# The first MLP pieces by token tile, means ahead of variances, bias transposes ahead: one change at the seam between attention and MLP of batch 0

## The chip, the cores and the metric

The kernel runs on one core of a Trainium2 chip. The metric is the device time of one execution in microseconds (us). The comparison of before and after is by medians over several runs; the profile describes one execution.

## The reference, cut to what matters

Attention over 8 batches of 8 heads, 576 positions, 64 wide, with a causal mask and a bias that comes from a running sum over `s`; then, for each token of 512 values, a LayerNorm, a two-layer MLP (512 to 2048 to 512, ReLU between) and a residual sum.

```python
scores = scale * q @ k.T                       # (8, 8, 576, 576)
cum = np.cumsum(np.maximum(s, 0.0), axis=-1)
bias = -(cum[:, :, :, None] - cum[:, :, None, :])
scores = np.where(causal, -1e9, scores + np.minimum(bias, 0.0))
x = softmax(scores) @ v                        # heads side by side: (8, 576, 512)
mu, var = x.mean(-1), ((x - mu) ** 2).mean(-1)
xn = (x - mu) / np.sqrt(var + 1e-6) * g_ln
out = x + np.maximum(xn @ w_ch1, 0.0) @ w_ch2
```

## The kernel before, in words

**Order of the work.** One loop over the 64 heads, `n = 8 b + h` (L732), is written out by hand: the schedule is manual, each engine runs its instructions in the order in which the loop issues them, and a semaphore wait of one instruction holds back all behind it on that engine. A step of the loop issues the scores of head `n` on TensorE (`scores`, L300: three PSUM tiles `sa`, `sb`, `sc`, each followed by an exponential on ScalarE into `er`; `scores_d`, L337, for every second head the small corner tile `sd`), two or more MLP "units" of the batch before (`run_units`, L544), and the product with `v` of an earlier head (`pv_next`, L717, which runs `pv`, L374: 15 small matmuls into `pot`, then a reciprocal and two scalings on VectorE into `xb` and `xm`). In steps 0 to 7 there is no MLP work yet, since batch 0 has to be complete first. `keep_warm` (L552) issues matmuls on zeros into a tile `idle`; nothing uses them.

**MLP units.** `batch_units` (L526) makes 32 units for each batch: 16 of `mlp1` (L480), which take 128 of the 2048 hidden columns each, four matmuls of 128x128 weights `w_bf` by 512 tokens `xT` into a tile `ph`, and a ReLU into `hT` on ScalarE (or on VectorE for the first unit of a step); then 16 quarters of `mlp2` (L498) into `py`, where each fourth one ends with the scaling by `rstd`, the residual sum into `yo` and the store.

**LayerNorm.** `ln_stats` (L414) takes partial statistics of the finished heads' columns; `ln_xn` (L439) merges them for one token tile (`bn_aggr` into `mv`) and makes `xn = (x - mean) * g`; with `on_pool` the two steps of `xn` run on GpSimd (`xc`, then `xn`). The division by the deviation is not in `xn`: it is applied after `mlp2` through `rstd`, which works since ReLU lets a positive factor through. `ln_tr` (L465) transposes `xn` on TensorE (`trx`) and copies it to `xT`. For batch 0, `pv_next` at its last head runs all four tiles: tile 3 on GpSimd, tiles 0 to 2 on VectorE, then `rstd`. Step 8 (L757) issues the scores of head 8, one warm-up matmul, all four `ln_tr`, then three units of all 512 tokens.

**Queries and keys.** For the first three batches they come as pairs of heads: `ld_cast_pair` (L129, GpSimd's DMA queue) loads them as `kp` and `qp`, `tr_pair` (L239) transposes them on TensorE into `trqk`, `evac_pair` (L258) copies them into `kq`, the keys on VectorE and the queries on ScalarE, two copies each. The table `PAIRS` (L659) says at which step which pair is made; in steps from 9 on, `qk_pair` (L271) stands behind the first two units. Pair `g` serves heads `2g` and `2g + 1`: pair 5 made in step 9 serves head 10 on.

**The bias rows.** `bias_rows` (L221) transposes the running sums to token-major form, 15 small transposes into `trc` and four copies on ScalarE into `cT`, at step 12. `cT` is first read by `cast_rows` at step 19.

**PSUM.** Pool `ps_s` holds three banks (`sa`, `sb`, `sc`), `ps_m` two (`ph`, `py`, and `trqk` up to pair 4), `ps_t` two (`trx`, `sd`, `idle`, later `trqk`, and `pot` of batch 0's odd heads), `ps_o` one (`pot`).

**GpSimd's queue** also issues the weight loads: `pre` (L662) places the loads of pairs 6 and 7 and of two quarters of `w2` at step 8, the other two quarters at step 10. Behind them stand the causal selects (`affine_select`, L327) of heads from 10 on.

Of the kernel before, what the change touches and what calls it, by code (L numbers as in the profile page):

```python
# [9 lines left out]
F32 = mybir.dt.float32  # L10
BF16 = mybir.dt.bfloat16
# [4 lines left out]
P = 128  # L16
# [3 lines left out]
def kernel(  # L20
# [54 lines left out]
    hT = const.tile([P, FB, 512], BF16, name="hT")  # L75
    gb = const.tile([P, Dm], F32, name="gb")
    rstd = const.tile([P, B, NT], F32, name="rstd")
    mhalf = const.tile([P, 8], F32, name="mhalf")
    v_bf = [const.tile([P, NT, H, D + 1], BF16, name=f"v_bf{i}") for i in range(2)]

# [137 lines left out]
                in_=src[0:m, :].unsqueeze(1).to_broadcast([m, G - a, S]),  # L218
            )

    def bias_rows():  # L221
        tr = ps_t.tile([P, 3, NT, BH], BF16, name="trc", tag="tr")
        for j, src in enumerate((c_hi, c_mid, c_lo)):
            for t in range(NT):
                pn = P if t < NF else TL
                nc.tensor.transpose(
                    tr[0:pn, j, t, :], src[:, t * P : t * P + pn], ident[0:BH, 0:BH]
                )
        for t0, t1, pn in ((0, NF, P), (NF, NT, TL)):
# [4 lines left out]
            nc.scalar.copy(out=cT[0:pn, t0:t1, 1, :, 0], in_=tr[0:pn, 0, t0:t1, :])  # L234


    trs = {}
# [186 lines left out]
    xTs = {}  # L424
    xns = {}

    done = {}
# [5 lines left out]
    def ln_rstd(b):  # L433
        n = len(x_tiles(b))
        rs = rstd[:, b, 0:n]
        nc.vector.tensor_scalar_add(out=rs, in0=mvs[b][:, 0:n, 1], scalar1=1e-6)  # L436
        nc.gpsimd.tensor_tensor(out=rs, in0=rs, in1=mhalf[:, 0:n], op=ALU.pow)  # L437

    def ln_xn(b, t, on_pool=False):  # L439
        tiles = x_tiles(b)  # L440
        if t >= len(tiles):
            return
        nc.vector.bn_aggr(out=mvs[b][:, t, :], in_=st[b][:, t, 0 : 4 if b == 0 else 3, :])  # L443
        xn = xnp.tile([P, Dm], BF16, name="xn", tag="xn")
        if on_pool:
            xc = yop.tile([P, Dm], F32, name="xc", tag="yo")
            nc.gpsimd.tensor_scalar(
                out=xc, in0=tiles[t], scalar1=mvs[b][:, t, 0:1], scalar2=None, op0=ALU.subtract
            )
            nc.gpsimd.tensor_tensor(out=xn, in0=xc, in1=gb, op=ALU.mult)  # L450
        else:
            nc.vector.scalar_tensor_tensor(  # L452
                out=xn,
                in0=tiles[t],
                scalar=mvs[b][:, t, 0:1],
                in1=gb,
                op0=ALU.subtract,
                op1=ALU.mult,
            )
        xns[b, t] = xn  # L460
        done[b] = done.get(b, 0) + 1
        if done[b] == len(tiles):
            ln_rstd(b)

    def ln_tr(b, t, eng="dve"):  # L465
        if (b, t) not in xns:
            return
        xn = xns.pop((b, t))
        tr = ps_t.tile([P, KD, P], BF16, name="trx", tag="tr")
        for kd in range(KD):  # L470
            nc.tensor.transpose(tr[:, kd, :], xn[:, kd * P : (kd + 1) * P], ident)  # L471
# [80 lines left out]
    def keep_warm(n):  # L552
        w = ps_t.tile([P, 512], F32, name="idle", tag="tr")
        for _ in range(n):
            nc.tensor.matmul(w, lhsT=zeros[:, 0:P], rhs=zeros, start=True, stop=True)
# [99 lines left out]

    PAIR_LOADS = {12: 8, 13: 9, 14: 10, 17: 11}
    PAIRS = {9: 5, 11: 6, 13: 7, 14: 8, 15: 9, 16: 10, 21: 11}  # L659


    def pre(n):  # L662
        if n == 0:
            nc.vector.memset(mhalf, -0.5)
            ld_cast_pair(4)
        elif n == 1:
            ld_w1(1)
        elif n == 3:
            ld_cast_pair(5)
            for t in range(NT):  # L670
                ld_cast_v(1, t)
        elif n == 4:
            ld_w1(2)
            ld_w1(3)
        elif n == 8:
            ld_cast_pair(6)
            ld_w2(0)
            ld_cast_pair(7)
            ld_w2(1)
        elif n == 10:  # L680
            ld_w2(2)
            ld_w2(3)
        elif n == 12:
            bias_rows()
            nc.vector.memset(cT[:, :, 0, :, 0], -1.0)
            nc.vector.memset(cT[:, :, 1, :, 1:4], 1.0)
        elif n == 16:
            for r in rows:
                nc.gpsimd.memset(r[:, :, :, KA:P], 0.0)
        if n in PAIR_LOADS:  # L690
            ld_cast_pair(PAIR_LOADS[n])
        if n % 4 == 0 and 2 <= n // 4 + 1 < 2 * NPE:
            aug(n // 4 + 1, nc.sync)
        for gam in range(2 * NPE, NG):
            m = n - 4 * gam
            if m == -6:
                ld_rows(gam, 0), ld_rows(gam, 1)
            elif m == -5:
                cast_rows(gam, 0), cast_rows(gam, 1)
                ld_rows(gam, 2), ld_rows(gam, 3)  # L700
            elif m == -4:
                tr_rows(gam, 0), tr_rows(gam, 1)
                cast_rows(gam, 2), cast_rows(gam, 3)
                ld_rows(gam, 4)
            elif m == -3:
                tr_rows(gam, 2), tr_rows(gam, 3)
                cast_rows(gam, 4)
            elif m == -2:
                tr_rows(gam, 4)
        for nb in range(2, B):  # L710
            m = n - H * nb + (5 if nb == 2 else 7)
            if 0 <= m < NT:
                ld_v(nb, m)
            if 1 <= m <= NT:
                cast_v(nb, m - 1, "pool")

    def pv_next():  # L717
        pb, ph_ = pend.pop(0)
        pv(pb, ph_)
        if ph_ in (3, 5) or (ph_ == 7 and pb > 0):  # L720
            ln_stats(pb, ph_ // 2 - 1)
        elif pb == 0 and ph_ in (6, 7):
            ln_stats(0, ph_ - 4)
        if ph_ == 7:
            ln_open(pb)
            if pb == 0:
                ln_xn(0, 3, True)
            for t in range({0: 3, 1: 2, B - 1: 1}.get(pb, NT)):
                ln_xn(pb, t)


    for n in range(BH):  # L732
        b, h = n // H, n % H
        pre(n)
        if n < 8:
            scores(b, h)
            if h in (1, 3, 5, 6):
                scores_d(b, h // 2)
            if h in (0, 2, 4):
                qk_pair(h // 2 + 1, ("dve", "dve"), ("act", "dve" if h < 4 else "act"))  # L740
            pend.append((b, h))
            if n == 7:
                pv_next()
                tr_pair(4)
                pv_next()
                evac_pair("k", 4, ("act", "act"))
                evac_pair("q", 4, ("act", "act"))
                keep_warm(4)
                continue
            if n % 2 == 1 or n == 0:  # L750
                keep_warm(2)
            if n > 1:
                pv_next()
            if n == 6:
                pv_next()
            continue
        if n == 8:  # L757
            scores(b, h)
# [12 lines left out]
        run_units(1, True)  # L771
        if h % 2 == 0:
            scores_d(b, h // 2)
        run_units(1)
        if n in PAIRS:
            qk_pair(PAIRS[n], ("dve", "dve"), ("act", "act"))
        if n > 9:
            pv_next()
        pend.append((b, h))
        lt = {2: (0, 1), 3: (2, 3, 4)}.get(h, ()) if b > 1 else ()  # L780
        for t in lt:
            ln_tr(b - 1, t)
            if t != 1 and t != 4:
                run_units(1)
                nu -= 1
        if n == 2 * H + 2:
            for t in range(2, NT):
# [46 lines left out]
```

## Time and profile before

| | before |
|---|---|
| median of 13 runs | 378.62 us (377.14 to 381.52) |
| the profiled execution: device time | 378.97 us |
| its span in the trace | 377.2 us |
| mean granted TensorE clock | 0.982 |
| TensorE (PE) busy with matmuls | 362.5 us, 96% of the span |
| VectorE (DVE), ScalarE (ACT), GpSimd (POOL) busy | 205.4, 194.1, 166.1 us |
| bytes moved by DMA | 50.42 MB |

How to read the lines of the trace that follow below: a line of the timeline gives start and duration in us, then engine, source line, operation, output and inputs by the program's names, shapes and a count; `x4` is four instructions merged, and the duration then runs from the first one's start to the last one's end. In brackets stands how long the engine had been idle just before and what ended it. A single matmul shows its whole passage through the array (some 0.2 to 0.4 us), of which the next one overlaps most: prices are taken from start to start. A line of the stages gives, for each stretch, its length, the busy time of PE, weight loads, DVE, ACT and POOL with counts, the granted clock (1.00 is full), and DMA.

### The profile page before, as it was taken

Reading aid. Unit: us, or ns where it says so; the run is one execution under the profiler, and the core shown is the slowest. Engines: PE = TensorE matmul, PEld = TensorE weight load, DVE = VectorE, ACT = ScalarE, POOL = GpSimd, SP = SyncE. Lnnn points to the kernel's source line nnn. Section 1 sums busy time; section 2 is a strip of 40 time slices with the busy share of each in tenths; the row PEclk is TensorE's granted clock in tenths of the full one; section 3 lists DMA queues with packets and bytes.
Section 4 is the critical chain, followed back from the end, with each engine's and each line's share of the span. In section 5 each row is a group of like instructions: output and inputs, shape, how many; then the busy total and the mean of one; then the engine's idle time right before and its main releaser. Section 6 shows DMA issues by size and latency. Waiting matters only on the chain.

```text
span 377.2 us, 8267 instructions
## 1 busy us (share of the span) xinstructions
PE 362.5 (96%) x3028; PEld 198.4 (53%) x3028; DVE 205.4 (54%) x535; ACT 194.1 (51%) x371; POOL 166.1 (44%) x443
## 2 busy tenths in 40 slices
PE   8995888999999999999999999999999999999995
PEld 3673455655555555555555555555555554444444
DVE  7696255978535754584348545853485574212211
ACT  5896657953873277327732773277327713411510
POOL 8856446644662465536473656364652201000000
PEclk9997888999999999999999999999999999999999
DMA  8999998148986499849887989397930011002013
GB/s 143 173 186 156 157 169 138 19 89 205 202 196 126 118 235 194 191 107 229 173 206 147 224 198 184 92 252 166 197 104 28 2 43 71 1 30 83 0 30 84
DMA packets 147981, 50.42 MB, mean 134 GB/s; under 512 B 134185, under 2 KB 143268, under 8 KB 147940
## 3 DMA queue, kind: packets, MB, share of 16 engines
q1 hardware_dynamic: 129364, 40.74, 48.5%
q0 software_dynamic: 18176, 8.62, 19.8%
q10 hardware_dynamic: 400, 0.52, 0.5%
q8 instruction: 24, 0.39, 0.5%
q14 instruction: 17, 0.14, 0.1%
HBM read 37.11 MB, written 9.44 MB: 123 GB/s over the span
## 4 chain that ended last, share of the span: by engine, by line
PE 86%; DVE 8%; ACT 3%; DMA 2%; issue 1%
PE ph L484 34%; PE py L502 30%; PE pot L385 7%; PE sa L308 3%; PE sc L308 3%; PE sb L308 3%; DVE xn L452 3%; PE trx L471 2%; ACT kq L97 2%; DVE stats L419 1%; DMA kq<-c 1%; DMA c_in<-in_s_dram 1%; PE trqk L251 1%; DVE xb L395 1%; DVE mv L443 1%
## 5 line engine op out<-in xcount | busy, mean ns | idle before, releaser
L502 PE MATMUL py<-w_bf,hT 128*128 128x512 bf16 (+1 forms) x592 | 136.4, 373 | 0.4 <-DVE yo L511 0.4
L484 PE MATMUL ph<-xT,w_bf 128*128 128x512 bf16 x512 | 125.6, 388 | 0.6 <-DVE xT L99 0.6
L494 ACT ACTIVATE hT<-ph 128x512 bf16<-128x512 f32 x105 | 62.7, 597 | 70.7 <-PE ph L484 70.7
L484 PEld LDWEIGHTS <-w_bf 128*128 128x128 bf16 x576 | 52.6, 99 | 56.1 <-issue 7.6
L502 PEld LDWEIGHTS <-hT 128*128 128x128 bf16 x592 | 53.5, 98 | 49.3 <-issue 0.9
L319 ACT ACTIVATE er<-sa 128x512 bf16<-128x512 f32 x64 | 38.1, 596 | 78.6 <-PE sa L308 48.2
L327 POOL TENSOR_SCALAR_AFFINE_SELECT er<-er 128x128 bf16<-128x128 bf16 x216 | 59.3, 298 | 35.0 <-ACT er L319 34.5
L492 DVE TENSOR_SCALAR hT<-ph 128x512 bf16<-128x512 f32 x39 | 27.0, 692 | 65.6 <-PE ph L484 59.2
L175 POOL CAST rows<-rowtmp 128x512 bf16<-128x512 f32 (+1 forms) x50 | 30.5, 610 | 47.7 <-DMA rowtmp<-in_q_dram 45.1
L308 PEld LDWEIGHTS <-kq 68*128 68x128 bf16 x440 | 33.0, 98 | 29.4 <-DVE kq L99 2.7
L385 PEld LDWEIGHTS <-er 128*128 128x128 bf16 x960 | 38.0, 99 | 13.4 <-issue 1.5
L385 PE MATMUL pot<-v_bf,er 128*128 128x65 bf16 x960 | 40.5, 195 | 0.1
L393 DVE RECIPROCAL rinv<-pot 128x5 f32<-128x5 f32 x64 | 12.3, 193 | 51.4 <-PE pot L385 51.0
L319 ACT ACTIVATE er<-sc 128x512 bf16<-128x512 f32 x64 | 38.9, 609 | 0.0
L319 ACT ACTIVATE er<-sb 128x512 bf16<-128x512 f32 x64 | 38.2, 596 | 0.0
L511 DVE SCALAR_TENSOR_TENSOR yo<-py,rstd,xb 128x512 f32<-128x512 f32 x32 | 23.9, 748 | 23.9 <-PE py L502 19.2
L308 PE MATMUL sa<-kq 68*128 68x512 bf16 x64 | 24.8, 387 | 5.3 <-ACT kq L97 4.7
L395 DVE TENSOR_TENSOR xb<-pot,rinv 128x256 f32<-128x256 f32 x64 | 27.2, 425 | 2.2
L437 POOL TENSOR_TENSOR rstd<-rstd,mhalf 128x4 f32<-128x4 f32 (+1 forms) x8 | 8.8, 1098 | 39.2 <-DVE rstd L436 39.2
L452 DVE SCALAR_TENSOR_TENSOR xn<-xb,mv,gb 128x512 bf16<-128x512 f32 x31 | 25.3, 816 | 1.1
L101 POOL CAST v_bf<-vtmp 128x512 bf16<-128x512 f32 (+1 forms) x30 | 18.4, 615 | 16.8 <-DMA vtmp<-in_v_dram 14.6
L419 DVE BATCH_NORM_STATS2 stats<-xb 128x6 f32<-128x128 f32 (+2 forms) x100 | 25.3, 312 | 0.4
(95 smaller groups left out, 326.4 us busy)
## 6 DMA issues: line engine op xcount, KB each, us to landing
out_dram<-yo SPq DMA_DIRECT2D x32, 256.0 KB
vtmp<-in_v_dram SPq DMA_DIRECT2D x24, 256.0 KB
rowtmp<-in_k_dram SPq DMA_DIRECT2D x40, 128.0 KB
rowtmp<-in_q_dram SPq DMA_DIRECT2D x40, 128.0 KB
w_bf<-in_moe_w_ch_dram POOLq DMA_DIRECT2D x8, 512.0 KB, 10.4
kp<-in_k_dram POOLq DMA_DIRECT2D x11, 144.0 KB, 4.5
qp<-in_q_dram POOLq DMA_DIRECT2D x11, 144.0 KB, 4.5
v_bf<-in_v_dram POOLq DMA_DIRECT2D x8, 128.0 KB, 8.4
```

The lines of the kernel that those rows point to most:

```text
L175: nc.gpsimd.tensor_copy(out=r[0:pn, :, :, 0:D], in_=loaded.pop(("rows", gam, t))[0:pn])
L308: nc.tensor.matmul(a[:, c + a0 - q0 : c + a1 - q0], lhsT=k_cols(b, h, kb), rhs=cols, start=True, stop=not (pe_mask and diag),)
L319: nc.scalar.activation(out=e[:, o : o + 512], in_=a, func=ACT.Exp, scale=scale)
L327: nc.gpsimd.affine_select(out=e[:, o : o + P], in_=e[:, o : o + P], compare_op=ALU.is_ge, fill=0.0, base=0, pattern=[[1, P]], channel_mult ...
L385: nc.tensor.matmul(pot[:, t, :], lhsT=e[:, o : o + P], rhs=vv[:, kb, h, :], start=(kb == 0), stop=(kb == last),)
L395: nc.vector.tensor_tensor(out=xb[b][:, :, hs], in0=pot[:, 0:NF, 0:D], in1=rinv[:, 0:NF].unsqueeze(2).to_broadcast([P, NF, D]), op=ALU.mult,)
L419: nc.vector.bn_stats(out=st[b][:, t, part, :], in_=x[:, lo:hi])
L452: nc.vector.scalar_tensor_tensor(out=xn, in0=tiles[t], scalar=mvs[b][:, t, 0:1], in1=gb, op0=ALU.subtract, op1=ALU.mult,)
L484: nc.tensor.matmul(ph, lhsT=w1_bf[:, kd, fb * P : (fb + 1) * P], rhs=xT[:, kd, :], start=(kd == 0), stop=(kd == KD - 1),)
L492: nc.vector.tensor_scalar_max(out=hT[:, fb, :], in0=ph, scalar1=0.0)
L494: nc.scalar.activation(out=hT[:, fb, :], in_=ph, func=ACT.Relu)
L502: nc.tensor.matmul(py[0], lhsT=hT[:, fb, t * P : (t + 1) * P], rhs=w2_bf[:, fb, c0:c1], start=(fb == 0), stop=(fb == FB - 1),)
```

## The change

1. **Batch 0's norm.** `ln_first` (new) makes the means of its four tiles in one step from the partial statistics: three small VectorE operations (`cm`, a reduction, a scaling into `mean0`), then the four `xn` on VectorE. `ln_first_rstd` (new) issues the four `bn_aggr` and `rstd` later, behind the ReLUs of the first four units. GpSimd makes no `xn` any more.
2. **Step 8.** The first four `mlp1` pieces are computed one token tile at a time: `columns(t)` issues, for each of four `ph` tiles, four matmuls of 128 tokens. It follows the transposes with a lag of one tile. Two of the four `ph` take the banks of `ps_m`, two take banks of `ps_s`. The scores of head 8 come behind all of it, then one unit instead of three.
3. **Bias rows.** The 15 transposes move from step 12 to the end of step 7, into the bank of `ps_o`; the four copies into `cT` move from ScalarE at step 12 to VectorE at the end of step 9. The first product with `v` that uses `ps_o` again is that of head 8, in step 10.
4. **Step 7** ends with eight warm-up matmuls instead of four.
5. **Pairs.** In steps from 9 on `qk_pair` stands ahead of the scores instead of behind the units. The loads of pairs 8 to 11 come one step earlier, those of pairs 6 and 7 and of two quarters of `w2` at step 7 instead of 8.
6. **Batch 1.** Three of its five `xn` are made with its last head instead of two; the copies of its `trx` go to ScalarE.

```diff
-    def bias_rows():
-        tr = ps_t.tile([P, 3, NT, BH], BF16, name="trc", tag="tr")
+    def bias_tr():
+        tr = ps_o.tile([P, 3, NT, BH], BF16, name="trc", tag="pot")
...
+    def bias_rows(tr):
         for t0, t1, pn in ((0, NF, P), (NF, NT, TL)):
-            nc.scalar.copy(
+            nc.vector.tensor_copy(
...
+    def ln_first():
+        parts = st[0][:, 0:NF].rearrange("p t c (e x) -> p t (c e) x", x=3)
+        cm = small.tile([P, NF, 8], F32, name="cm", tag="cm", bufs=1)
+        nc.vector.tensor_tensor(out=cm, in0=parts[:, :, :, 0], in1=parts[:, :, :, 1], op=ALU.mult)
+        nc.vector.tensor_reduce(out=mean0, in_=cm, axis=AX.X, op=ALU.add)
+        nc.vector.tensor_scalar_mul(out=mean0, in0=mean0, scalar1=1.0 / Dm)
+        for t in range(NF):
+            ln_xn(0, t)
...
-    PAIR_LOADS = {12: 8, 13: 9, 14: 10, 17: 11}
+    PAIR_LOADS = {11: 8, 12: 9, 13: 10, 16: 11}
...
-        elif n == 8:
+        elif n == 7:
             ld_cast_pair(6)
             ld_w2(0)
             ld_cast_pair(7)
...
-                keep_warm(4)
+                trc = bias_tr()
+                keep_warm(8)
                 continue
...
+            phs = [
+                pool.tile([P, 512], F32, name="ph", tag=tag)
+                for pool, tag in ((ps_m, "m"), (ps_m, "m"), (ps_s, "s"), (ps_s, "s"))
+            ]
+            def columns(t):
+                cols = slice(t * P, (t + 1) * P)
+                for fb, ph in enumerate(phs):
+                    for kd in range(KD):
+                        nc.tensor.matmul(
+                            ph[:, cols],
+                            lhsT=w1_bf[:, kd, fb * P : (fb + 1) * P],
+                            rhs=xTs[0][:, kd, cols],
+                            start=(kd == 0),
+                            stop=(kd == KD - 1),
+                        )
+            for t in range(NF):
+                ln_tr(0, t, "act" if t < 3 else "dve")
+                if t > 0:
+                    columns(t - 1)
+            columns(NF - 1)
...
+            ln_first_rstd()
+            queue += batch_units(0)[4:]
             scores(b, h)
             scores_d(b, h // 2)
             pend.append((b, h))
-            keep_warm(1)
-            for t in range(NF):
-                ln_tr(0, t, "act" if t < 3 else "dve")
-            queue += batch_units(0)
-            run_units(3)
+            run_units(1)
             continue
...
+        if n in PAIRS:
+            qk_pair(PAIRS[n], ("dve", "dve"), ("act", "act"))
         scores(b, h)
...
-        if n in PAIRS:
-            qk_pair(PAIRS[n], ("dve", "dve"), ("act", "act"))
         if n > 9:
             pv_next()
+        if n == 9:
+            bias_rows(trc)
```

How the instructions stand on ScalarE from the last copies of step 7 on, before the change (`er<-sa` is an exponential, `xT<-trx` the copy of a transposed token tile, `hT<-ph` a ReLU, `kq<-trqk` the copies of a query pair):

```order
L97 COPY kq_103<-trqk 64x2x288 x4
L319 ACTIVATE er<-sa 128x512
L319 ACTIVATE er<-sb 128x512
L319 ACTIVATE er<-sc 128x512
L354 ACTIVATE er<-sd 64x2x64
L97 COPY xT<-trx 128x4x128 x3
L494 ACTIVATE hT<-ph 128x512 x3
```

And in the changed kernel, up to the exponentials of head 9:

```order
L98 COPY kq_104<-trqk 64x2x288 x4
L98 COPY xT<-trx 128x4x128 x3
L797 ACTIVATE hT<-ph 128x512 x2
L323 ACTIVATE er<-sa 128x512
L323 ACTIVATE er<-sb 128x512
L323 ACTIVATE er<-sc 128x512
L358 ACTIVATE er<-sd 64x2x64
L507 ACTIVATE hT<-ph 128x512
L98 COPY kq_104<-trqk 64x2x288 x2
```

The exponentials of head 8 moved behind the token tiles' copies and two ReLUs, and the copies of pair 5 (the last row) moved ahead of the exponentials of head 9.

On VectorE, from the last tile's norm of batch 0 to the first scaling of a `pot` of batch 1, before the change:

```order
L443 BN_AGGR mv<-stats 128x2
L452 SCALAR_TENSOR_TENSOR xn<-xb,mv,gb 128x512
L436 TENSOR_SCALAR rstd<-mv 128x4
L99 COPY xT<-trx 128x4x128
L492 TENSOR_SCALAR hT<-ph 128x512
L99 COPY kq_103<-trqk 64x2x288 x2
```

And in the changed kernel the same stretch:

```order
L469 TENSOR_SCALAR mean_100<-mean_100 128x4
L451 SCALAR_TENSOR_TENSOR xn<-xb,mean_100,gb 128x512 x4
L100 COPY xT<-trx 128x4x128
L799 TENSOR_SCALAR hT<-ph 128x512 x2
L442 BN_AGGR mv<-stats 128x2 x4
L438 TENSOR_SCALAR rstd<-mv 128x4
L100 COPY kq_104<-trqk 64x2x288 x2
L505 TENSOR_SCALAR hT<-ph 128x512
L234 COPY cT<-trc 128x4x64x3
L238 COPY cT<-trc 128x4x64
```

The four `xn` stand together with no `bn_aggr` between them, the variances come behind two ReLUs, and the copies of the bias rows have joined this engine.

On GpSimd's queue, from the last loads of `w1` to the first causal select, in the changed kernel:

```order
L198 DMA w_bf<-in_moe_w_ch_dram 128x4x512 x2
L128 DMA kp<-in_k_dram 96x2x384
L128 DMA qp<-in_q_dram 96x2x384
L201 DMA w_bf<-in_moe_w_ch_dram 128x4x512
L439 TENSOR_TENSOR rstd<-rstd,mhalf 128x4
L201 DMA w_bf<-in_moe_w_ch_dram 128x4x512 x2
L331 AFFINE_SELECT er<-er 128x128 x4
```

Between the fourth and the fifth of these rows stand a second `kp`, `qp` and a quarter of `w2`, in the same words. Before the change all of these loads stood behind `rstd`; now six of them stand ahead of it.

More of the change, by code (lines that the diff above doesn't have):

```diff
@@ L437, in ln_rstd, with ln_aggr, ln_xn @@
         nc.gpsimd.tensor_tensor(out=rs, in0=rs, in1=mhalf[:, 0:n], op=ALU.pow)
-    def ln_xn(b, t, on_pool=False):
+    def ln_aggr(b, t):
+        nc.vector.bn_aggr(out=mvs[b][:, t, :], in_=st[b][:, t, 0 : 4 if b == 0 else 3, :])
+    def ln_xn(b, t):
         tiles = x_tiles(b)
@@ L726, in pv_next @@
             if pb == 0:
-                ln_xn(0, 3, True)
-            for t in range({0: 3, 1: 2, B - 1: 1}.get(pb, NT)):
+                ln_first()
+                return
+            for t in range({1: 3, B - 1: 1}.get(pb, NT)):
                 ln_xn(pb, t)
@@ L786 @@
         if n == 2 * H + 2:
-            for t in range(2, NT):
+            for t in range(3, NT):
                 ln_xn(1, t)
```

46 lines of the change are left out of this document (24 added, 22 removed).

## The prediction

> **What bounds the kernel now.** I read TensorE's busy time by stages first, then its granted clock, then its timeline from 27 us on. From head 18 on PE is never idle and runs at full clock:
>
> ```profile
> 70.00:75.00 5.00, 5.00 (x56) 3.02 (x54) 4.75 (x12) 4.81 (x9) 3.58 (x10) 1.00 0.01 4
> 120.00:140.00 20.00, 20.00 (x182) 11.27 (x180) 13.54 (x35) 9.67 (x20) 9.33 (x26) 1.00 0.76 181
> ```
>
> So each microsecond by which PE reaches head 17 earlier, with the same work behind it, moves the end. The losses lie before that, between 28 and 78 us:
>
> ```profile
> 26.84 0.34 PE L385 MATMUL pot<-v_bf,er 128*128 128x65 bf16 x6
> ...
> 27.53 0.73 PE L385 MATMUL pot<-v_bf,er 128*128 128x65 bf16 x15
> 28.09 1.03 PE L555 MATMUL idle<-zeros 128*128 128x512 bf16 x4
> 30.88 0.38 PE L308 MATMUL sa<-kq 68*128 68x512 bf16 x1 [1.77 <-ACT kq L97]
> ...
> 32.34 0.38 PE L471 MATMUL trx<-ident,xn 128*128 128x128 bf16 x4
> ...
> 34.59 1.04 PE L471 MATMUL trx<-ident,xn 128*128 128x128 bf16 x8 [1.02 <-DVE xn L452]
> 36.23 4.85 PE L484 MATMUL ph<-xT,w_bf 128*128 128x512 bf16 x12 [0.61 <-DVE xT L99]
> ...
> 45.91 0.38 PE L308 MATMUL sa<-kq 68*128 68x512 bf16 x1 [1.70 <-ACT kq L97]
> ...
> 55.20 1.14 PE L226 MATMUL trc<-ident,c 64*128 64x64 bf16 x15 [1.24 <-ACT kq L97]
> ...
> 77.92 0.38 PE L308 MATMUL sa<-kq 68*128 68x512 bf16 x1
> ```
>
> The reader sees PE standing for ScalarE's copies of a query pair (three times) and for the norm, and twelve unit matmuls in 4.85 us: 0.40 apiece, twice what they take elsewhere. The granted clock (the column ahead of the DMA share) says why:
>
> ```profile
> 33.00:34.00 1.00, 0.38 (x4) 0.21 (x4) 0.96 (x2) 1.00 (x3) 0.98 (x1) 0.84 1.26 212
> 47.00:48.00 1.00, 1.00 (x6) 0.44 (x5) 0.25 (x1) 0.98 (x3) 0.61 (x3) 0.66 1.26 209
> 50.00:51.00 1.00, 1.00 (x11) 0.60 (x9) 0.58 (x2) 0.35 (x2) 0.00 (x0) 0.63 1.23 204
> 57.00:58.00 1.00, 1.00 (x6) 0.39 (x4) 0.70 (x1) 1.00 (x5) 0.00 (x0) 0.78 1.26 245
> 60.00:61.00 1.00, 1.00 (x17) 0.81 (x15) 0.10 (x1) 0.60 (x1) 1.00 (x4) 0.51 0.22 32
> ```
>
> A mean of 0.84 is full clock up to 33.68 and half of it after; likewise the switches at 47.32, 50.74, 57.56 and 60.98. All lie on one grid of 3.41 us, so the clock is set window by window; the first cold stretch ended two windows on, at 40.5.
>
> **Prices on PE**, from a step that had no wait inside it (head 14):
>
> ```profile
> 65.58 0.38 PE L308 MATMUL sa<-kq 68*128 68x512 bf16 x1 [1.23 <-ACT kq L97]
> ...
> 66.22 1.03 PE L484 MATMUL ph<-xT,w_bf 128*128 128x512 bf16 x4
> 67.09 0.22 PE L343 MATMUL sd<-kq 68*128 68x64 bf16 x2
> ...
> 68.02 0.42 PE L251 MATMUL trqk<-ident,kp 96*128 96x96 bf16 x6
> ...
> 68.53 0.61 PE L385 MATMUL pot<-v_bf,er 128*128 128x65 bf16 x15
> 68.98 0.38 PE L308 MATMUL sa<-kq 68*128 68x512 bf16 x1
> ```
>
> Scores 0.64, unit 0.87 (0.217 a matmul), corner 0.06, pair 0.51, product with v 0.45. A transpose of `trx` costs (0.38 - 0.22) / 3 = 0.054 from start to start, with 0.22 for the last one's passage as in the corner's row.
>
> **The loss before.** From 28.09 to head 17's scores at 77.92 are 49.8 us. The work in it: nine heads' scores 6.2 (two of them with four mask matmuls at 0.054), five corners 0.3, 21 units 18.3, 16 `trx` 0.9, six pairs 3.1, `trc` 1.1, seven products 3.2: 33.1. Loss 16.7: waits 1.9 (28.96 to 30.88) and 4.2 (1.70, 1.24, 1.23), the norm 3.0 (32.34 to 36.23 less 0.9), dummies 0.9, half clock 2.1 + 1.7 + 1.7 (half of 36.23 to 40.5 and of two windows), 1.2 in small pieces.
>
> **The change, part by part.** The other engines' prices:
>
> ```profile
> 28.24 0.27 DVE L402 TENSOR_SCALAR xm<-pot,rinv 64x64 f32<-64x64 f32 x1
> ...
> 29.68 0.58 DVE L419 BATCH_NORM_STATS2 stats<-xb 128x6 f32<-128x64 f32 x4
> ...
> 30.72 1.18 DVE L452 SCALAR_TENSOR_TENSOR xn<-xb,mv,gb 128x512 bf16<-128x512 f32 x1
> ...
> 32.11 0.75 DVE L452 SCALAR_TENSOR_TENSOR xn<-xb,mv,gb 128x512 bf16<-128x512 f32 x1
> ...
> L443 DVE BATCH_NORM_AGGREGATE mv<-stats 128x2 f32<-128x24 f32 x4 | 0.9, 243 | 0.0
> L436 DVE TENSOR_SCALAR rstd<-mv 128x4 f32<-128x4 f32 x4 | 0.6, 162 | 0.0
> L492 DVE TENSOR_SCALAR hT<-ph 128x512 bf16<-128x512 f32 x39 | 27.0, 692 | 65.6 <-PE ph L484 59.2 <-ACT er L319 5.2 <-PE sd L343 0.9
> 63.66 0.80 DVE L99 COPY kq<-trqk 64x576 bf16<-64x576 bf16 x1 [0.43 <-PE trqk L251]
> 30.67 1.57 POOL L447 TENSOR_SCALAR xc<-xb,mv 128x512 f32<-128x512 f32 x1 [3.61 <-DVE mv L443]
> 27.59 3.24 ACT L97 COPY kq<-trqk 64x576 bf16<-64x576 bf16 x4
> 33.02 1.17 ACT L97 COPY xT<-trx 128x512 bf16<-128x512 bf16 x2
> 66.05 0.60 ACT L319 ACTIVATE er<-sa 128x512 bf16<-128x512 f32 x1 [0.52 <-PE sa L308]
> 67.50 0.27 ACT L354 ACTIVATE er<-sd 64x128 bf16<-64x128 f32 x1
> 68.22 0.60 ACT L494 ACTIVATE hT<-ph 128x512 bf16<-128x512 f32 x1 [0.45 <-PE ph L484]
> ```
>
> *Bias transposes and dummies.* `trc` now needs `ps_o`, which head 6's `pot` leaves at 28.51: 0.4 lost. It ends at 29.6; eight dummies cost 1.7, to 31.3. Nobody waits for these: `xn` is not there yet.
>
> *Norm.* Statistics end at 30.26. Three small operations replace the first `bn_aggr`. The trace has no such reduction: between 3 x 0.16 and 3 x 0.24, I take 0.5 by the 4-element row, to 30.8. The four `xn` follow at 0.75; the 1.18 lay beside GpSimd's `xc`, which goes. They end at 31.55, 32.3, 33.05, 33.8. PE waits 0.3 for the first.
>
> *Token tiles.* Transposes at 31.6 and 32.35, the first copy 0.59 on ACT, columns from 32.65: 64 matmuls at 0.054 are 3.5, two more transposes 0.4, to 36.55. The norm's tail is covered; 0.6 is lost. Before, the units began at 36.23 at half clock.
>
> *Head 8's scores.* Two `ph` hold `ps_s`; ACT frees one after two ReLUs, DVE the other after two of 0.69: 0.7 lost. Behind them on ACT stand all later exponentials, which start at 37.4 instead of 31.4; they serve products in step 10 (45 us), so this costs nothing.
>
> *Pairs first.* The three copy waits (4.2) go: a scores call and two units (2.4) now lie between a pair's transposes and its reader. What is late next is ACT. In a step with a pair it needs 1.45 for three exponentials, 1.62 for copies, 0.6 for a ReLU, in even steps 0.27: 3.67 to 3.94, against 3.34 to 3.40 on PE. Five such steps (9, 11, 13 to 15) lose 0.33 to 0.54 each: 1.7 to 2.7, I take 2.5 since the copies now stand ahead of the exponentials. Step 16 has four units and covers it.
>
> *`cT` on DVE.* 1280 elements a partition by the 0.80 of 576: 1.8, at 42 to 44, ahead of the product that waits for `ps_o` at 45. Cover 1 us.
>
> *Loads.* Six move ahead by a step; a pair is needed 8 us or more after its issue. Four `bn_aggr` (1.0) lie behind the ReLUs, where DVE is free. Batch 1's `xT` copies move to ACT, idle by then: nothing.
>
> Loss after: 0.4 + 1.7 + 0.3 + 0.6 + 0.7 + 2.5 = 6.2, no half clock. The two additional units (five at step 8 instead of three) are work done early, not a loss. Lead 16.7 - 6.2 = 10.5. A check from DVE, full at 70 to 75 (4.75 of 5): its work from pair 7 (63.66) to head 17 stays, and by this sum pair 7 stands at 53.1, 10.6 earlier, so the lead cannot grow behind it. I take off 1.0 for waits my sum does not see: 9.5. The profiled execution took 378.97 (span 377.2), near the median of 378.62: **369.5**. With half of the unsure losses gone it is 366.5; with both clock windows and the loads against it, 374.5.
>
> **Which windows stay warm.** Cold followed 1.41 us of matmuls (45.91 to 47.32, 41%); the window to 30.27 had 0.18 + 1.43 (47%) and stayed warm. The window to 57.56 had 1.3 of matmuls and 1.1 of `trc`, together 70%, and went cold: transposes did not count. The Trainium skill ("TensorE: Matmul & The Clock Gate", Part 4) says that transpose-mode does not count as busy in the same way; by that, the trace agrees, and the moved `trc` warms nothing. In the changed kernel the poorest windows, around 28.1 to 31.5 and 31.3 to 34.7, hold 1.73 of dummies or of columns: 51%.
>
> **The rivals.**
>
> *Cold columns.* If the norm comes 0.3 later, the second window falls to 42% and the columns run at half clock: 3.5 more, 373.0. The margin is small, but the window must also fall just there: 0.12.
>
> *Weights bound the narrow matmuls.* Each has its own weight load:
>
> ```profile
> L484 PEld LDWEIGHTS <-w_bf 128*128 128x128 bf16 x576 | 52.6, 99 | 56.1 <-issue 7.6
> ```
>
> At 99 ns apiece the columns cost 64 x 0.045 = 2.9 more, 372.4. Against it: `trx` has new weights each time and goes at 54 ns, `pot` at 30. The same page ("Back-to-back issue gap") gives about 81 ns for pairs of load and 128 columns; by that it would be 371.2, and the trace disagrees. 0.04.
>
> *Loads set the pace.* Heads 11 to 16 come up to 13 us earlier than before, their pairs and `w2` only by what GpSimd's queue allows. Three late pairs at 1 us each give 372.5; were all of the lead given back later, 379.0. 0.10 and 0.03.
>
> *Slower: GpSimd's queue.* It waited 1.85 us for an earlier load to land before it could issue one:
>
> ```profile
> 25.48 1.58 POOL L197 DMA_DIRECT2D w_bf<-in_moe_w_ch_dram  x2 [1.85 <-DMA w_bf<-in_moe_w_ch_dram]
> DMA to landing us min/median/max: 7.7/10.4/14.0
> ```
>
> Six loads now stand ahead of `rstd` and of head 10's selects, which PE needs at 51 (step 12). Each microsecond beyond 51 is lost; past 61.5 the kernel is slower, at 65 it takes 382.5. That asks for a wait of 36 us after the last `w1` issue, where the longest landing is 14.0. 0.05.
>
> **Chances.** Forecast 0.66, cold 0.12, weights 0.04, loads 0.10, given back 0.03, slower 0.05. All but the last two end below 377.5, so faster by over 0.3% (1.1 us, about what a measurement of this kernel can tell from no change) has 0.92, the same 0.03, slower 0.05. The range 366.5 to 374.5 takes in the first four.
>
> **What would show it.** Right: no stage below full clock from 28 to 78 us; first columns near 32.7 at 0.054 each; head 9's scores near 39.7; head 17's near 69; no PE wait for `kq` copies of over 0.5. Wrong: a clock of 0.5 anywhere in 33 to 70, columns at 0.08 or more, a PE wait on a DMA of `kp` or `w_bf`, selects of head 10 after 51, or new idle time of PE behind 80 us.

## The result, and the profile after

| | before | after |
|---|---|---|
| median | 378.52 us (48 runs, 374.25 to 381.52) | 368.14 us (11 runs, 367.76 to 368.29; a twelfth on record, not in the median, took 368.94) |
| ratio | | 0.9733, 95% interval 0.9713 to 0.9754 |
| the profiled execution: device time, span | 378.97, 377.2 us | 368.28, 366.6 us |

The changed kernel is 10.4 us faster; forecast were 9.5, 369.5 us. Two of the profiled executions of the experiments below lose more at their start, ahead of everything that was changed: TensorE waits 1.8 and 2.6 us there for a late transfer of bias rows (0.5 before, 0.8 after) and then runs at half clock for a while; where this happened, it is said.

First the page of the changed kernel, busy times and the granted clock in 40 slices; the clock is full everywhere, and PE is busy for 5.0 us less than the 362.5 of before with the same work and three dummies more (eight in step 7 instead of four, none in step 8 instead of one), since no matmul runs at half speed.

```profile
PE 357.5 (98%) x3079; PEld 197.9 (54%) x3079; DVE 205.4 (56%) x539; ACT 194.2 (53%) x371; POOL 161.7 (44%) x441
...
PEclk9999999999999999999999999999999999999999
```

Two of the stages of one microsecond that were cold before, with the granted clock ahead of the DMA share:

```profile
33.00:34.00 1.00, 1.00 (x22) 1.00 (x19) 0.64 (x1) 0.39 (x1) 0.83 (x2) 1.00 1.22 200
47.00:48.00 1.00, 1.00 (x7) 0.41 (x5) 0.99 (x2) 0.97 (x2) 0.31 (x1) 1.00 1.24 212
```

TensorE's waits, as sum, number and longest; the waits of scores and of `trc` on the copies of a query pair are gone, and 0.6 us in which the corner `sd` waits for such copies are left; the 0.8 on a transfer lies at 13 us, ahead of the change:

```profile
PE sa L312 <- DMA kq<-c: 0.8, 1, 0.8
PE sd L347 <- ACT kq L98: 0.6, 2, 0.4
PE trx L484 <- DVE xn L451: 0.5, 2, 0.3
...
PE sb L312 <- ACT hT L797: 0.2, 1, 0.2
```

TensorE's timeline over the changed part, to be laid beside that of before:

```profile
27.47 0.73 PE L389 MATMUL pot<-v_bf,er 128*128 128x65 bf16 x15
28.50 1.16 PE L227 MATMUL trc<-ident,c 64*128 64x64 bf16 x15 [0.31 <-DVE xm L406]
29.59 1.90 PE L568 MATMUL idle<-zeros 128*128 128x512 bf16 x8
31.71 0.40 PE L484 MATMUL trx<-ident,xn 128*128 128x128 bf16 x4 [0.22 <-DVE xn L451]
32.38 0.40 PE L484 MATMUL trx<-ident,xn 128*128 128x128 bf16 x4 [0.26 <-DVE xn L451]
32.78 1.05 PE L782 MATMUL ph<-xT,w_bf 128*128 128x128 bf16 x16
...
36.80 0.38 PE L312 MATMUL sa<-kq 68*128 68x512 bf16 x1
...
38.45 1.02 PE L497 MATMUL ph<-xT,w_bf 128*128 128x512 bf16 x4
...
39.82 0.38 PE L312 MATMUL sa<-kq 68*128 68x512 bf16 x1
...
56.06 0.38 PE L312 MATMUL sa<-kq 68*128 68x512 bf16 x1
...
58.15 0.22 PE L347 MATMUL sd<-kq 68*128 68x64 bf16 x2 [0.40 <-ACT kq L98]
...
59.89 0.41 PE L255 MATMUL trqk<-ident,kp 96*128 96x96 bf16 x6 [0.21 <-ACT er L358]
60.44 0.41 PE L255 MATMUL trqk<-ident,qp 96*128 96x96 bf16 x6
60.69 0.38 PE L312 MATMUL sa<-kq 68*128 68x512 bf16 x1
...
69.00 0.38 PE L312 MATMUL sa<-kq 68*128 68x512 bf16 x1
```

Head 9's scores start at 39.82 instead of 40.91 although the units behind which they stand are two more, and head 17's at 69.00 instead of 77.92. That is 8.92, and with two units more done by then (1.74) a lead of 10.66: the two spans differ by 10.6. Nothing was given back behind head 17.

VectorE's part of it:

```profile
30.24 0.20 DVE L467 TENSOR_TENSOR cm<-stats 128x32 f32<-128x32 f32 x1
...
30.90 2.74 DVE L451 SCALAR_TENSOR_TENSOR xn<-xb,mean,gb 128x512 bf16<-128x512 f32 x4
...
42.39 0.95 DVE L234 COPY cT<-trc 128x768 bf16<-128x768 bf16 x1
...
44.07 0.28 DVE L238 COPY cT<-trc 64x64 bf16<-64x64 bf16 x1
...
56.98 1.41 DVE L423 BATCH_NORM_STATS2 stats<-xb 128x6 f32<-128x256 f32 x4
58.31 0.41 DVE L423 BATCH_NORM_STATS2 stats<-xm 128x6 f32<-128x256 f32 x1
58.75 1.64 DVE L100 COPY kq<-trqk 64x576 bf16<-64x576 bf16 x2
```

### The profile page after: what moved, and what is told of

Its sections match the earlier page's. It is cut to its first block, busy times and chain, and to the rows that moved or that the text cites. A ratio compares the mean times of both kernels' runs of the same rounds, so it can differ in the third digit from the quotient of the medians.

```text
span 366.6 us, 8372 instructions
## 1 busy us (share of the span) xinstructions
PE 357.5 (98%) x3079; PEld 197.9 (54%) x3079; DVE 205.4 (56%) x539; ACT 194.2 (53%) x371; POOL 161.7 (44%) x441
## 4 chain that ended last, share of the span: by engine, by line
PE 84%; DVE 6%; ACT 3%; POOL 2%; DMA 2%; issue 1%; ACTq 0%; POOLq 0%
PE ph L497 32%; PE py L515 31%; PE pot L389 7%; PE sc L312 3%; PE sb L312 3%; PE sa L312 3%; DVE xn L451 2%; PE trx L484 2%; DMA v_bf<-in_v_dram 2%; ACT er L323 2%; ACT kq L98 1%; DVE stats L423 1%; POOL v_bf L147 1%; PE trqk L255 1%; PE ph L782 1%
## 5 line engine op out<-in xcount | busy, mean ns | idle before, releaser
L497 PE MATMUL ph<-xT,w_bf 128*128 128x512 bf16 x496 | 117.8, 379 | 0.1
L507 ACT ACTIVATE hT<-ph 128x512 bf16<-128x512 f32 x102 | 61.0, 598 | 62.8 <-PE ph L497 62.8
L497 PEld LDWEIGHTS <-w_bf 128*128 128x128 bf16 x560 | 50.3, 97 | 51.7 <-issue 3.3
L389 PEld LDWEIGHTS <-er 128*128 128x128 bf16 x960 | 37.4, 98 | 14.2 <-issue 0.7
L389 PE MATMUL pot<-v_bf,er 128*128 128x65 bf16 x960 | 39.7, 193 | 0.2
L312 PE MATMUL sc<-kq 68*128 68x256 bf16 (+1 forms) x208 | 25.2, 232 | 0.3
```

The source lines that it names most:

```text
L312: nc.tensor.matmul(a[:, c + a0 - q0 : c + a1 - q0], lhsT=k_cols(b, h, kb), rhs=cols, start=True, stop=not (pe_mask and diag),)
L389: nc.tensor.matmul(pot[:, t, :], lhsT=e[:, o : o + P], rhs=vv[:, kb, h, :], start=(kb == 0), stop=(kb == last),)
L497: nc.tensor.matmul(ph, lhsT=w1_bf[:, kd, fb * P : (fb + 1) * P], rhs=xT[:, kd, :], start=(kd == 0), stop=(kd == KD - 1),)
L507: nc.scalar.activation(out=hT[:, fb, :], in_=ph, func=ACT.Relu)
```

## The experiments

Theory A is the prediction's: the waits, the half-speed windows and the norm are separate terms, all ahead of head 17, which add up there. Against it stand C (everything comes from step 8, the later waits only pass it on) and, term by term, the rivals in the expectations.

**One part alone: pairs ahead, in the kernel before.**

```diff
+        if n in PAIRS:
+            qk_pair(PAIRS[n], ("dve", "dve"), ("act", "act"))
         scores(b, h)
...
-        if n in PAIRS:
-            qk_pair(PAIRS[n], ("dve", "dve"), ("act", "act"))
```

> The kernel before with one part of the change: the pair transposes and copies stand ahead of the scores. Theory A (waits and cold windows are separate terms that add): the three copy waits of 4.2 us go and with them the two half-speed windows behind them (1.7 each), while ScalarE's pace, as measured in the changed kernel, takes 2.2 back, and up to 1.8 more since the bias copies are still ScalarE's in step 12: 373.1 to 374.9 us. Theory C (all of the gain comes from step 8 and its norm, later waits are only passed on): 378.5. In the trace A expects no PE wait on a query copy ahead of scores, and full clock from 44 to 75 us; the units of step 8 stay at half clock.

Measured: 373.16 us (372.40 to 373.51), ratio 0.9846 (0.9815 to 0.9877): the low end of A; C is out, since nothing of step 8 was changed here. The only wait on a query copy that is left is the one at step 8, and the only cold stretch (33.2 to 40.0) is the one around the norm:

```profile
PE sa L308 <- ACT kq L97: 1.8, 1, 1.8
```

```profile
36.00:37.00 1.00, 1.00 (x4) 0.36 (x3) 0.00 (x0) 0.00 (x0) 1.00 (x2) 0.50 0.65 83
47.00:48.00 1.00, 1.00 (x17) 0.75 (x14) 0.92 (x4) 0.63 (x2) 0.07 (x1) 1.00 1.27 210
```

The 1.8 that I had set aside for the bias copies on ScalarE did not come.

**All but that part: pairs behind, in the changed kernel** (the same lines of the diff, the other way).

> The changed kernel with the pairs put back behind the two units, the rest kept. Theory A: 368.1 + 4.2 of copy waits + 3.4 of half-speed windows - 2.2 of ScalarE's pace = 373.5 us. If the waits return but no window goes cold (their place against the window grid is another): 370.1. Theory C (the gain is step 8's): 368.1 to 368.6.

Measured: 371.10 us (370.67, 370.91, 371.29 and 372.93). The three waits are back to within a hundredth (1.70, 1.25, 1.23), but no stage of the profiled execution is below full clock, though 43 to 44 has 0.04 us of PE in it:

```profile
PE sa L312 <- ACT kq L98: 4.2, 3, 1.7
```

```profile
43.00:44.00 1.00, 0.04 (x1) 0.13 (x2) 0.97 (x2) 0.88 (x2) 0.00 (x0) 1.00 1.26 214
```

So the part is worth 5.4 in the kernel before and 3.0 here. From the bias transposes to head 17 the profiled execution takes 43.44 us (28.16 to 71.60) against 40.50: 4.2 of waits and 1.0 of small pieces in the steps with a pair, for the 2.2 that these steps lose with the pairs ahead. My 373.5 was wrong in taking the cold windows as part of the waits: the same waits need not cost a window. That it depends on where the grid of windows cuts the work is the likely reason; it is argued, not shown. The one run with 372.93 has a mean clock of 0.993 where the others have 0.999 or more, which fits one cold window in that run alone.

**The clock alone: matmuls on zeros in the waits of the kernel before.**

```diff
-                keep_warm(4)
+                keep_warm(8)
...
                 ln_tr(0, t, "act" if t < 3 else "dve")
+                if t in (0, 1, 3):
+                    warm_o(4 if t < 3 else 2)
...
+        if n in (10, 14):
+            warm_o(5)
         scores(b, h)
...
+            warm_o(5)
             bias_rows()
```

> The kernel before with warm-up matmuls added where TensorE waits: eight instead of four at the end of step 7, four behind the first and second and two behind the last of the norm's transposes, five ahead of the scores of steps 10 and 14 and of the bias transposes of step 12, in the bank of ps_o that is free there. No wait is removed; only the clock is held. Theory A (half clock is a term of its own, 2.1 + 1.7 + 1.7): 378.6 - 5.5 = 373.1 us, plus up to 0.6 where the dummies outlast a wait: 373.1 to 373.7, full clock from 28 to 75 us, the waits as long as before. Rival (ScalarE and VectorE set the pace, so a faster TensorE only waits longer): 376 to 378.5.

Measured: 378.82 us (376.09 to 382.30 in ten runs), by the median no gain. The ten fall into two groups: five with a mean clock of 1.000 took 376.09 to 377.40, which is 1.1 to 2.4 less than before, and five at 0.986 to 0.990 took 380.23 to 382.30. As a test of theory A it is spoiled: the bank of `ps_o` is not free in steps 12 and 14, and the dummies, with all behind them, waited 4.0 us for VectorE. At full clock 5.5 won and 4.0 lost would be 377.0, inside the first group:

```profile
PE idle_o L555 <- DVE xm L402: 4.0, 2, 2.0
```

Again, then, with the dummies of steps 10, 12 and 14 in a bank of `ps_m` (`warm_m(5)` in place of `warm_o(5)` at these three).

> The kernel before with the same added warm-up matmuls as in the run with 378.82 us, but those of steps 10, 12 and 14 in a bank of ps_m: in the bank of ps_o they had to wait 4.0 us for the scaling of the product ahead of them, and the work behind waited with them. No wait of the kernel before is removed; only the clock is held. Theory A (half clock is a term of its own, 5.5 us): 378.6 - 5.5 = 373.1 us, up to 0.6 more where the dummies outlast a wait. Rival (the other engines set the pace, a faster TensorE waits longer): 376 to 378.5 at full clock.

Measured: 373.57 us (372.96 to 375.48), ratio 0.9867 (0.9839 to 0.9894), five of six runs at a clock of 0.999 or more. The waits stay, partly filled by dummies, as at step 10:

```profile
41.30 1.24 PE L560 MATMUL idle_m<-zeros 128*128 128x512 bf16 x5
43.17 0.38 PE L308 MATMUL sa<-kq 68*128 68x512 bf16 x1 [0.62 <-ACT kq L97]
```

Half clock was a term of its own: 5.0 us recovered of the 5.5 of the prediction, with up to 0.6 allowed for dummies that outlast a wait. The rival (a faster TensorE only waits longer) is out.

**Two dummies instead of eight, in the changed kernel** (`keep_warm(2)` for `keep_warm(8)`).

> The changed kernel with two warm-up matmuls instead of eight at the end of step 7. Nobody waits for these, so by the sum they cost nothing and only hold the clock. If the window from about 28 to 31.5 us then goes cold, with 0.4 us of dummies instead of 1.7 in it, the narrow columns run at half clock for one window or two: 1.7 to 3.5 us more, 369.9 to 371.6, clock 0.5 somewhere in 31 to 38 us, and a spread between runs above 1 us. Rival (the clock has margin to spare, the dummies do nothing): 368.1.

Measured: 369.54, 370.84 and 372.40 us, ratio 0.9789 (0.9741 to 0.9837), and 375.21 us in the fourth, profiled execution, whose start was disturbed: it reaches `trc` 4.5 us late (32.96). Behind that its trace still shows what the six missing dummies do. The clock is full again from 21.8 on, then half from 35.4 to 42.2, two windows, and the columns go at (39.10 - 37.45) / 16 = 0.103 us apiece, 39.10 being where the next transposes start:

```profile
38.00:39.00 1.00, 1.00 (x13) 1.00 (x10) 0.10 (x1) 0.06 (x1) 0.00 (x0) 0.50 1.22 193
```

```profile
37.45 1.87 PE L782 MATMUL ph<-xT,w_bf 128*128 128x128 bf16 x16
```

From `trc` to head 17 it takes 42.97 us instead of 40.50. The three other runs have no trace, but mean clocks of 0.994, 0.990 and 0.990 where the changed kernel has 0.998 to 1.000. A window at half clock loses 1.7 of some 368 us, 0.0046 of the mean: by these, one window in the first and two in the others. So the prediction's rival of cold columns is what happens without these six matmuls; with them, by the mean clocks, it happened in none.

**The first four pieces as whole units again** (all four transposes, then for each `ph` four matmuls of 512 tokens).

```diff
             for t in range(NF):
                 ln_tr(0, t, "act" if t < 3 else "dve")
-                if t > 0:
-                    columns(t - 1)
-            columns(NF - 1)
+            for fb, ph in enumerate(phs):
+                for kd in range(KD):
+                    nc.tensor.matmul(ph, lhsT=w1_bf[:, kd, fb * P : (fb + 1) * P], rhs=xTs[0][:, kd, :], ...)
```

> The changed kernel with the first four pieces again as whole units of 512 tokens, behind all four transposes and copies; their banks, the order around them and the norm are kept. The last xn ends at 33.64, its transposes near 34.0, its copy near 34.6, four units of 0.87 end at 38.1 instead of 36.76: 1.3 us more. The window before them then holds transposes and no matmul: if it goes cold, 1.7 to 3.5 more. Theory A with the clock: 371.1 to 372.9 us; without the clock: 369.4. Rival (the tile order is hidden anyway): 368.1.

Measured: 369.76 us (369.51 to 370.22), ratio 0.9760 (0.9730 to 0.9789): 1.6 more, the case without the clock (369.4). TensorE now waits for the last tile and its copy:

```profile
34.34 3.61 PE L782 MATMUL ph<-xT,w_bf 128*128 128x512 bf16 x16 [0.61 <-DVE xT L100]
```

Between the last dummy (about 31.1) and 34.34 there is no matmul but transposes, 3.2 us, and still every stage has a clock of 1.00.

**Means tile by tile** (no `cm`, no common step; `bn_aggr` ahead of each `xn`, all on VectorE).

```diff
-        if b > 0:
-            ln_aggr(b, t)
+        ln_aggr(b, t)
...
-            scalar=mvs[b][:, t, 0:1] if b > 0 else mean0[:, t : t + 1],
+            scalar=mvs[b][:, t, 0:1],
```

> The changed kernel with the four means made tile by tile again (one bn_aggr of about 0.2 us ahead of each xn, all on VectorE), no common step for the means; rstd stays behind the ReLUs. Theory A (what the norm gains is tile 3's way off GpSimd and the short units behind the first tile, not the common step): the first xn is out 0.24 + 0.67 after the statistics instead of 0.66 + 0.67, so 0.4 earlier, the last at the same time, and TensorE is the slower one from the second tile on: 367.7 us. Rival (the common step is what brings the tiles early, as it is written): 0.4 to 1.0 slower, 368.5 to 369.1.

Measured: 367.82 us (367.73 to 368.26 in six runs) against 368.14 (367.76 to 368.29): the ranges overlap, but the trace shows the step. The first transpose no longer waits, the second does, and from `trc` to head 17 it takes 40.12 us (28.38 to 68.50) instead of 40.50:

```profile
31.20 0.39 PE L475 MATMUL trx<-ident,xn 128*128 128x128 bf16 x4
32.04 0.40 PE L475 MATMUL trx<-ident,xn 128*128 128x128 bf16 x4 [0.45 <-DVE xn L449]
```

The common step for the means brings nothing. Of the short units the run above shows 1.6; the way of tile 3 off GpSimd, and head 8's scores behind the columns, were not tried by themselves.

**Bias transposes and copies back at step 12, on ScalarE** (`bias_rows(bias_tr())` in `pre(12)`, `ps_t` and `nc.scalar.copy` as before).

> The changed kernel with the bias transposes back at step 12 and their four copies back on ScalarE, the rest kept. Theory A (ScalarE paces steps 11 to 15): TensorE pays 0.9 for 15 transposes where it has nothing to wait for, and the copies (0.80 + 0.74 + 0.41 + 0.29 with overlap, 1.8 us together) fall into steps in which ScalarE has 0.3 us to spare, so 1.3 to 1.8 come on top: 370.3 to 370.9 us, with PE waits on ScalarE in steps 12 to 14 as the mark. If a window goes cold where the transposes stood before, 1.7 more. Rival (ScalarE's copies are hidden): 369.0.

Measured: 369.23 and 369.73 us at a mean clock of 1.000 and 0.998, 371.96 and 373.30 at 0.995 and 0.991 (the last with a disturbed start). At full clock this is nearer to the rival (369.0) than to A: 1.1 to 1.6 more, against 0.9 forecast for TensorE's own part. Step 11 is longer by the transposes, 4.03 us to head 12 instead of 2.84, and the later steps together by nothing:

```profile
49.96 0.38 PE L312 MATMUL sa<-kq 68*128 68x512 bf16 x1
...
52.90 1.16 PE L227 MATMUL trc<-ident,c 64*128 64x64 bf16 x15
53.99 0.39 PE L312 MATMUL sa<-kq 68*128 68x512 bf16 x1
```

A's price for ScalarE's copies was wrong: in step 12 it makes no pair, and has room for them. Step 12 is 0.21 longer than in the changed kernel (3.81 for 3.60), and step 14 is 0.23 shorter. The clock, though, suffers: without `trc` the dummies start 3.7 us ahead of the first transposes (30.10 to 33.78) instead of 2.1, and a window over the columns can go cold, as it did in the profiled execution (35.2 to 38.6).

**The loads back at their old steps** (`PAIR_LOADS = {12: 8, 13: 9, 14: 10, 17: 11}`, `elif n == 8` in `pre`).

> The changed kernel with the loads of pairs 6 to 11 and two quarters of w2 back at their old steps, behind rstd on GpSimd's queue. Theory A (pair 6 is needed at 45.76 us now): its two loads are issued near 40.0 and 40.7 and land 7.1 us later by the median, 12.8 at most, near 47.8 to 53: 2.0 us late at the median, 370.1 us, up to 6 more than that at the worst landing, with a PE wait of trqk on the DMA of kp or qp. Rival (the loads have slack, as the sum's term of nothing reads): 368.1.

Measured: 368.34 us (368.03 to 369.39), the same. A's expectation rested on a misreading: with `rstd` behind the units of step 8, `pre(8)` still stands ahead of it on GpSimd's queue, and pair 6 is issued as early as in the changed kernel (27.77):

```profile
28.10 0.64 POOL L128 DMA_DIRECT2D kp<-in_k_dram  x1 [0.38 <-PE trqk L255]
```

Only pairs 8 to 11 are loaded later; in the profiled execution (369.39) one of their transfers was late:

```profile
57.25 0.43 PE L255 MATMUL trqk<-ident,qp 96*128 96x96 bf16 x6 [0.67 <-DMA qp<-in_q_dram]
```

So the later loads of pairs 8 to 11 cost some cover and no time otherwise. The six loads of the changed kernel's step 7 stayed where they were in this run, so what they are worth wasn't tried.

**Where the pairs' steps still lose: pair 7 one step earlier** (`12: 7` for `13: 7`).

> The changed kernel with pair 7 made in step 12 instead of 13, the rest kept. Steps 13, 14 and 15 each carry a pair now, and step 14 loses 1.23 us to ScalarE and VectorE, which reach it late. Theory A (the copies queue up over neighbouring steps, so where the pairs stand decides): step 13 is left without copies, step 14 loses 0 to 0.4, step 12 may lose 0.4: 367.2 to 367.8 us. Rival (the losses go by the number of pairs, wherever they stand): 368.1.

Measured: 368.86 us (368.55 to 371.01). It is no gain: step 14 keeps 1.0 of its 1.23, and step 12, with a pair behind the one of step 11, has the same wait of the corner for a query copy:

```profile
51.83 0.22 PE L347 MATMUL sd<-kq 68*128 68x64 bf16 x2 [0.40 <-ACT kq L98]
```

**Pairs 8, 9 and 10 one step later** (`15: 8, 16: 9, 17: 10` for `14: 8, 15: 9, 16: 10`).

> The changed kernel with pairs 8, 9 and 10 one step later (15, 16 and 17 instead of 14, 15 and 16). Theory A: step 13 is followed by one without a pair, so step 14 no longer loses its 1.23; step 16 keeps about 0.3, step 17 has VectorE busy for 1.46 and ScalarE for 1.57 of 3.71 us and takes pair 10 for nothing: 366.8 to 367.2 us. Rival (the losses go by the number of pairs): 368.1.

Measured: 366.95 us (366.84 to 367.32, all four below all of the changed kernel's), ratio 0.9690 (0.9659 to 0.9722). Step 14 loses 0.20 instead of 1.23, and its corner no longer waits:

```profile
55.23 0.38 PE L312 MATMUL sa<-kq 68*128 68x512 bf16 x1
...
56.94 0.22 PE L347 MATMUL sd<-kq 68*128 68x64 bf16 x2
...
58.32 0.42 PE L255 MATMUL trqk<-ident,kp 96*128 96x96 bf16 x6
...
58.83 0.38 PE L312 MATMUL sa<-kq 68*128 68x512 bf16 x1
```

What lost in step 14 was not the number of pairs but pairs 8 and 9 in steps 14 and 15. In the changed kernel's trace, by the times at which each bank is released, the 1.23 are three waits for the two banks of `ps_t`. The corner at 58.15 (0.56 late) waits for the bank of pair 8's queries, which ScalarE has copied at 58.09. The key transposes of pair 9 at 59.89 (0.37 late) wait for the corner's exponential, which ScalarE ends at 59.84. The query transposes at 60.44 (0.30 late) wait for the keys of pair 8, which VectorE copies behind 1.8 us of statistics (56.98 to 58.75 above) and ends at 60.39:

```profile
56.48 1.61 ACT L98 COPY kq<-trqk 64x576 bf16<-64x576 bf16 x2
...
59.57 0.27 ACT L358 ACTIVATE er<-sd 64x128 bf16<-64x128 f32 x1
```

So 0.93 of the 1.23 is ScalarE's and 0.30 VectorE's. Moving pair 7 leaves the three waits nearly as they are; moving pairs 8 and 9 ends them.

**Both edits that measured faster.**

> The changed kernel with the two edits that measured faster than it together: means tile by tile (367.82 alone) and pairs 8 to 10 one step later (366.95 alone), against 368.14. Theory A (separate terms before head 17 add, since TensorE bounds all behind it): 368.1 - 0.3 - 1.2 = 366.6 us. Rival (what one edit wins the other waits for): 366.95 or more.

Measured: 366.75 us (366.47 to 367.38), ratio 0.9685 (0.9663 to 0.9707). From `trc` to head 17 its trace has 39.10 us (28.13 to 67.23), which is 40.50 less 0.38 of the one and 1.04 of the other: in the trace the two add. By time it can't be told from the run with the pairs alone.

## Why the prediction was right, by its steps

**The lead.** 16.7 lost before, 6.2 after: the difference of 10.5 was 10.66. From 28.03 to 69.00 the changed kernel has 34.8 us of work by the prediction's prices (the 33.1 of before and two units), so it loses 6.2:

| loss after (us) | forecast | measured |
|---|---|---|
| `ps_o` still held by `pot` | 0.4 | 0.5 |
| eight dummies | 1.7 | 1.7 |
| norm: first `xn` and column stage | 0.3 + 0.6 | 1.1 |
| banks of `ps_s` at head 8 | 0.7 | 0.7 |
| steps with a pair | 2.5 | 2.2 |

The first row is 28.50 - 28.03 (27.47 and the 0.56 from that product to the next instruction before the change); the third is 31.71 - 31.33 (29.59 and eight times 0.217), 32.38 - 31.93 (31.71 and four times 0.054), 32.78 - 32.60 and 0.1 up to 36.80; the fourth 38.45 - 36.80 less 0.91 of scores, masks and corner.

**The mis-sized term** is the allowance of 1.0 "for waits my sum does not see". In sum there were none: without it the sum says 378.97 - 10.5 = 368.5, and the profiled execution took 368.28. It is the whole miss in the profiled execution but 0.2. The upper end of the range was not added up right either: two windows (3.5) and the loads (3.0) on top of 369.5 make 376.0, not 374.5.

**Steps with a pair.** The engine was right, the place was not, and that the sums agree (2.2 for 2.5) is in part luck. I had put 0.33 to 0.54 into each of steps 9, 11 and 13 to 15, by ScalarE's total, and nothing into step 16. The odd steps lose nothing. What ScalarE is late with from steps 9 and 11 meets TensorE in steps 10 and 12, and steps 14 and 16 lose because they have a pair and a corner. Steps 10, 12, 14 and 16 lose 0.43, 0.20, 1.23 and 0.33 (step 14, to give one, takes 60.69 - 56.06 = 4.63 with pair 9 for 3.40 of work; the others start at 42.44, 49.11 and 64.04 and last 3.83, 3.60 and 4.96). In steps 10 and 12 TensorE stands at `sb` and `sc`, whose banks ScalarE's exponentials of the head before still read, in step 10 up to 43.24:

```profile
42.64 0.60 ACT L323 ACTIVATE er<-sc 128x512 bf16<-128x512 f32 x1
```

```profile
43.30 0.38 PE L312 MATMUL sc<-kq 68*128 68x320 bf16 x2
```

In steps 14 and 16 it is the two banks of `ps_t`, shared by `trqk` and the corner `sd`. By these ends ScalarE accounts for 1.9 of the 2.2, VectorE for 0.3, in step 14 alone. That ScalarE has more work than TensorE in one step is not yet a loss, as the bias copies at step 12 showed; it is one where TensorE's next tile needs a bank that ScalarE has yet to read.

**Clock.** Right in the sum: the run that only holds the clock recovers 5.0 of 5.5. What was not in the sum is that the number of cold windows of the kernel before differs from run to run: most of its runs have a mean clock of 0.982, but 374.68 us was measured at 0.995 and 380.81 at 0.977. That is part of the 7.3 us over which the runs of before spread, where the eleven of after spread over 0.5. Cold columns, given 0.12, did not happen. With six dummies gone they did, in the one run with a trace (2.5 us from `trc` to head 17) and, by the mean clocks, likely in the other three, at 1.4 to 4.3 us against the forecast 3.5.

**Norm.** The mean operations took 0.66 (30.24 to 30.90) instead of 0.5 and the four `xn` 2.74 instead of 3.0: they end at 33.64 (forecast 33.8), the columns start at 32.78 (32.65). The common means gain nothing: the first `xn` starts 0.69 us behind the last statistics where, with means tile by tile, it starts 0.20 behind them.

**The rest.** Columns go at (1.05 - 0.22) / 15 = 0.055 apiece, as forecast, so the rival of the weights is out. The exponentials of head 8 start at 37.34 (37.4). `cT` takes 1.96 from 42.39 to 44.35 (forecast 1.8), and the product that needs the bank comes at 45.30, so the cover was 0.95. No wait of TensorE on `kp`, `qp` or `w_bf` is in the trace, so loads neither set the pace nor gave the lead back. The slower case needed head 10's selects past 51; they start at 44.30:

```profile
44.30 0.30 POOL L331 TENSOR_SCALAR_AFFINE_SELECT er<-er 128x128 bf16<-128x128 bf16 x1 [3.05 <-ACT er L323]
```

## What to carry to other kernels

Where one engine is full from some point on, add up what it loses ahead of that point, in its own prices, and forecast the lead from that; an allowance for the unseen on top needs a row too. Fill a wait with idle matmuls only in a bank whose last reader is long done, or the filler itself becomes the wait. When copies pace a step, look which bank holds up whom and what else stands in the copying engine's queue before going by its total: three pairs moved one step later gained 1.2 us, another moved one step earlier lost 0.7.

## What the runs showed of the hardware that was not expected

The clock is set by windows on a grid of 3.41 us, and where the grid lies against the work differs from one execution to the next: the clock fell at 33.68 us in the kernel before, at 33.18 with pairs ahead, at 35.20 with the bias transposes at step 12 and at 35.40 with two dummies, which is 2.96, 2.46, 1.07 and 1.27 us behind a whole number of windows from the start of the span. In the kernel before the clock fell behind a window with 1.41 us of matmuls (41%) and not behind one with 1.61 (47%); with whole units in the changed kernel, 3.2 us without an ordinary matmul did not lower it once in four runs (mean clocks of 0.998 to 1.000). That such a stretch is split by the grid into two windows with enough work each would fit both; it is argued, since a window that stays warm leaves no mark in the trace. It would also take luck: for neither window to hold more than 1.8 to 2.0 us of the stretch, the grid has to cut it near its middle, by my estimate from these numbers in at most a quarter of its possible places, and it would have to do so four times out of four. So how much work keeps a window warm stays open. The Trainium skill ("TensorE: Matmul & The Clock Gate", the table under "Why this matters for your kernels") warns of idle gaps of more than about 3 us; by that the trace disagrees in part, since the waits of 1.2 to 1.7 us before the change were enough where they fell into one window.

Before the change VectorE's three `xn` took 1.18 us (beside GpSimd's `xc`), 0.75, and 1.47 (beside GpSimd's own `xn`, 32.33 to 33.99); without GpSimd's part all four take 2.74, as four times the 0.75 with some overlap. That GpSimd held VectorE up is the likely reason; no run tried it by itself.
